# A gated-MLP kernel after linear attention: one written order of steps replaced by another

## The chip, the core and the metric

One core of a Trainium2 chip runs the whole program. Its engines are TensorE (PE, matmuls), VectorE (DVE), ScalarE (ACT), GpSimd (POOL) and SyncE (SP), which issues every DMA here. The metric is device time of one execution in microseconds, lower is better.

## What is computed

Eight batches of 576 rows. The first half is attention without a score matrix: q is made a softmax over its 64 channels, k one over the 576 rows, k^T v is a 64x64 matrix for each of 8 heads, and x = q (k^T v). The second half is a gated MLP with a mixing of rows:

```python
kv = einsum('bhsd,bhse->bhde', softmax(k, axis=rows), v)
x = einsum('bhsd,bhde->bhse', softmax(q, axis=channels), kv)   # heads side by side: 576 x 512
h = gelu_tanh(x @ w_in)                                        # 576 x 1024
u, v = h[..., :512], h[..., 512:]
v_n = (v - mean(v)) / sqrt(var(v) + 1e-6) * g_ln
gated = u * (einsum('ts,bsd->btd', w_sg, v_n) + b_sg[None, :, None])
out = x + gated @ w_out
```

## The kernel before

Each large product is made in float32r from a high and a low part of each operand: three matmuls (high x high, low x high, high x low) that add up in PSUM. So every operand has a step that rounds it to the high part (ScalarE mostly) and one that subtracts to get the low part (VectorE or GpSimd).

The work is cut into 1167 small steps, and a text, PLAN (lines 46 to 133 from the point that matters here), lists them with their arguments: batch first, then tile, head or part, and a letter where the engine is chosen (V VectorE, A ScalarE, G GpSimd). A loop at the end calls them in that order, each by its name. Nothing else sets the order: `InOrder` (line 141) ties every instruction of VectorE, ScalarE, GpSimd and SyncE to the one before it on the same engine, and `mm` keeps TensorE's matmuls in the order of the text. Between engines there are only the waits that data and buffers need. A step that waits holds up everything behind it on its own engine.

The steps that this document speaks of, with the line of each:

- load_q, load_k, load_v, load_kt (387 to 399): DMA loads of one part of a batch. kt_max, kt_put, kt_get (402 to 415): the maxima of k over the rows, written to DRAM and read back in every partition. The loads of kt and kt_get take turns in two buffers (5 b + p, modulo 2).
- k_sub, k_exp (419, 425): k less its maxima, and the exponential. q_max, q_swapm, q_top, q_sub, q_exp, q_sum, q_swapd, q_inv, q_mul, q_turn (504 to 636): softmax of q and its transposition. q_max, q_top, q_sum, q_inv and q_turn are VectorE's.
- x_kv (685): first x_mm of a batch, 32 matmuls in three PSUM tiles, then kv_all of the next batch, whose matmuls read k and v; x_high, x_low, x_endh, x_endl (730 to 742) read the three tiles; kv_inv and kv_scale (671, 676) read kv_all's.
- hv_mm (747), hv_gelu, hv_sq, hv_stat, hv_pow, hv_norm, hv_high, hv_low (757 to 790): a 128-row tile of v, its GELU, its norm, high and low part. tail_high, tail_low, tail_again (799 to 808): the last 64 rows of a batch.
- hu_mm, hu_gelu (813, 818): one quarter of u. sg_mm (821), 28 matmuls: the mixing of rows for one quarter, which reads the high and low part of v of all tiles, in order. gate, gate_high, gate_low (830 to 837): u times that, its high and low part.
- out_mm (850), out_add, out_rest, out_store (856 to 866): the last product, the addition of x's high and low part, and the store. last_mm and what follows (873): the last quarter of the last batch in three column groups.
- wo_a, wo_b, wo_d, wo_h, wo_l (297 to 317) and ws_h, ws_l, b_h, b_l: the weights' high and low parts, w_out put together from 64-bit words by a scale, a shift and an OR. The raw words of w_out lie in the buffers that x_h and x_l of batch 1 take later.

PSUM has three double tiles that x_mm, hu_mm, sg_mm, out_mm and last_mm take in turn and two single ones for hv_mm and kv_all (`bank`, line 225). A step of the first kind cannot begin until the tile of three turns ago has been read: by gate on VectorE after a sg_mm, by out_add on VectorE after an out_mm, by hu_gelu on ScalarE after a hu_mm.

Of the kernel before, what the change touches and what calls it, by code (L numbers as in the profile page):

```python
# [59 lines left out]
hv_stat 1 0 A, hv_stat 1 1 A, q_sub 2 1, q_exp 2 1, gate 0 2, load_k 2 0, k_sub 2 0, hv_stat 1 2 A, hv_pow 1 2, q_sum 2 1, k_exp 2 0, sg_mm 0 0  # L60
gate 0 0, q_swapd 2 1, q_inv 2 1, q_mul 2 1 1, q_mul 2 1 0, sg_mm 0 1, hv_high 1 2, gate_high 0 2, load_kt 3 1, hu_mm 1 0, k_exp 2 1, kv_all 2
load_k 3 0, load_kt 3 2, hv_pow 1 0, gate 0 1, gate_high 0 1, gate_high 0 0, hv_stat 1 3, hv_pow 1 3, gate_high 0 3, hv_norm 1 3, gate_low 0 0
gate_low 0 1, gate_low 0 2, gate_low 0 3 G, q_max 2 0, hu_gelu 1 0, out_mm 0 1, hv_norm 1 0, wo_l 2 V, kt_max 3 1, kt_max 3 2, load_k 3 1, q_swapm 2 0
# [68 lines left out]
out_add 7 1, out_store 7 1, both 7 0, out_mm 7 0, out_add 7 0, out_store 7 0, last_mm 7 1, out_mm 7 2, out_add 7 2, last_add 7 1, out_store 7 2
last_store 7 1, last_mm 7 0, last_mm 7 2, last_add 7 0, last_store 7 0, last_add 7 2, last_store 7 2
"""


# [821 lines left out]
```

## Time and profile before

| | |
|---|---|
| median of 3 runs | 495.99 us (495.83 to 497.17) |
| profiled execution | 497.11 us, span 495.3 us, granted TensorE clock 1.0 throughout |
| TensorE matmul | 485.9 us busy, 98% of the span, 3885 matmuls |
| TensorE weight load | 447.3 us, 90% |
| VectorE | 338.9 us, 68%, 530 instructions |
| ScalarE | 244.4 us, 49% |
| GpSimd | 159.5 us, 32%, 173 instructions |
| DMA | 57.28 MB, mean 116 GB/s |

The engines' busy times overlap; idle time of an engine costs only where it holds up the one that ends last. Matmuls are pipelined, so each is shown longer (295 ns for 288 columns) than the distance to the next start (some 133 ns); a stop of TensorE is read from the starts, or from the idle time in brackets, which is shorter.

### The profile page before, as it was taken

What the parts mean: (1) busy time and instruction counts of PE and PEld (TensorE: products, weight loads), DVE (VectorE), ACT (ScalarE), POOL (GpSimd) and SP (SyncE); (2) the same over time, 40 slices, a digit from 0 to 9 for tenths busy, and PEclk for the clock granted to TensorE, in tenths of its full rate; (3) what the DMA queues carried; (4) which work ended last, traced back from release to release, by engine and by line L of the source; (5) the groups of instructions that cost most, each with busy time, mean ns of one, the idle gap of its engine ahead of it and who ended that gap; (6) DMA issues with size and microseconds to landing.
All of it is one profiled execution on the core that took longest, in us unless ns stands there. A gap on an engine that the chain in (4) does not pass through costs nothing.

```text
span 495.3 us, 9376 instructions
## 1 busy us (share of the span) xinstructions
PE 485.9 (98%) x3885; PEld 447.3 (90%) x3885; DVE 338.9 (68%) x530; ACT 244.4 (49%) x402; POOL 159.5 (32%) x173
## 2 busy tenths in 40 slices
...
GB/s 301 386 406 194 285 52 120 148 61 145 175 228 55 192 218 85 71 103 26 179 48 201 97 194 11 78 125 1 119 26 0 25 73 0 1 1 24 32 42 96
DMA packets 20637, 57.28 MB, mean 116 GB/s; under 512 B 3057, under 2 KB 3569, under 8 KB 20594
## 3 DMA queue, kind: packets, MB, share of 16 engines
...
q8 instruction: 30, 0.49, 0.4%
...
## 4 chain that ended last, share of the span: by engine, by line
PE 66%; DVE 14%; DMA 8%; POOL 5%; issue 3%; ACT 3%; SPq 1%; POOLq 0%; ACTq 0%; DVEq 0%
PE ps L238 66%; DVE o L151 2%; DMA kmt<-kt 2%; DVE qq L151 2%; DMA vv<-v 2%; DMA qq<-q 2%; DVE qd L151 2%; POOL qq L151 2%; POOL kk L151 1%; DVE qm L151 1%; DMA out<-o 1%; DMA eye<-identity 1%; ACT qq L151 1%; DVE vnl L151 1%; POOL o L151 1%
## 5 line engine op out<-in xcount | busy, mean ns | idle before, releaser
L238 PE MATMUL ps<-ulow,wo_h 128*128 128x288 f32 (+1 forms) x260 | 56.8, 296 | 0.5 <-DVE ulow L151 0.5
L238 PE MATMUL ps<-gh,wo_h 128*128 128x288 f32 (+1 forms) x260 | 56.6, 295 | 0.3 <-DVE o L151 0.3
L238 PE MATMUL ps<-gh,wo_l 128*128 128x288 f32 (+1 forms) x260 | 56.2, 293 | 0.0
L238 PE MATMUL ps<-ws_h,vnh 128*128 128x288 f32 x256 | 55.0, 296 | 0.0
L238 PE MATMUL ps<-ws_h,vnl 128*128 128x288 f32 x256 | 54.8, 295 | 0.0
L238 PE MATMUL ps<-ws_l,vnh 128*128 128x288 f32 x256 | 54.8, 295 | 0.0
L151 POOL TENSOR_TENSOR ulow<-u,gh 128x576 fp32r<-128x576 f32 x16 | 25.0, 1560 | 83.0 <-DVE ulow L151 53.8
L151 POOL TENSOR_TENSOR rs<-ve,half 128x1 f32<-128x1 f32 x36 | 25.9, 723 | 77.2 <-DVE ve L151 71.0
L151 ACT CAST gh<-u 128x576 fp32r<-128x576 f32 x32 | 20.9, 673 | 58.7 <-DVE u L151 58.6
L151 ACT ACT_TABLE_LOAD x34 | 43.6, 1283 | 9.7 <-PE ps L238 4.3
L151 DVE TENSOR_TENSOR u<-ps,u 128x576 f32<-128x576 f32 x32 | 23.8, 748 | 32.3 <-PE ps L238 32.3
L238 PE MATMUL ps<-x_h,wi_h 128*128 128x288 f32 (+2 forms) x256 | 42.1, 299 | 1.6 <-DVE o L151 1.3
L238 PEld LDWEIGHTS ps<-gh,wo_h 128*128 128x128 f32 x260 | 42.1, 188 | 1.1 <-DVE o L151 0.5
L238 PEld LDWEIGHTS ps<-ulow,wo_h 128*128 128x128 f32 x260 | 42.0, 188 | 0.9 <-DVE ulow L151 0.9
L238 PEld LDWEIGHTS ps<-ws_h,vnh 128*128 128x128 f32 x256 | 41.7, 188 | 0.7
L238 PEld LDWEIGHTS ps<-gh,wo_l 128*128 128x128 f32 x260 | 42.1, 188 | 0.0
L151 ACT ACTIVATE u<-ps 128x576 f32<-128x576 f32 (+2 forms) x36 | 21.0, 597 | 42.7 <-PE ps L238 39.0
L238 PEld LDWEIGHTS ps<-ws_h,vnl 128*128 128x128 f32 x256 | 41.3, 188 | 0.0
L238 PE MATMUL ps<-x_h,wi_l 128*128 128x288 f32 (+2 forms) x256 | 41.3, 296 | 0.0
L238 PEld LDWEIGHTS ps<-ws_l,vnh 128*128 128x128 f32 x256 | 41.3, 188 | 0.0
L238 PE MATMUL ps<-x_l,wi_h 128*128 128x288 f32 (+2 forms) x256 | 41.2, 295 | 0.0
L238 PE MATMUL ps<-wi_h,x_h 128*128 128x512 f32 x144 | 39.9, 399 | 0.6 <-ACT x_h L151 0.5
...
## 6 DMA issues: line engine op xcount, KB each, us to landing
...
```

The source lines that it names most:

```text
L151: ins = op(*args, **kw)
L238: tc.keep_in_program_order(nc.tensor.matmul(*args, **kw))
```

## The change

The text of PLAN is written anew from the 180th step on. The 179 steps ahead of it stay as they are, up to the first matmuls that transpose k of batch 1. The steps are the same 1167, each with the same arguments and the same engine; only their order differs, and with it the order of each engine's instructions. The words that came with it: order of the steps from batch 1's k^T v on made anew, with VectorE's two-SBUF-input instructions and GpSimd taking turns in order of time; nothing else. No wait or dependency is written into the kernel for that.

The diff has 90 lines of steps on either side. Those that this document speaks of:

```diff
@@ -46,91 +46,91 @@
-k0_copy 1 2, q_turn 1 2, hu0_mm 0 1 1, hu0_mm 0 1 0, k0_copy 1 3, hu0_gelu 0 1, ws_h 0, kv_mm 1 0, load_v 2 0, kv_inv 1 0, hu0_gelu 0 0, kv_mm 1 1
-load_k 2 1, kv_scale 1 0, kv_inv 1 1, kv_scale 1 1, load_q 2 1, x_mm 1, wo_b 0, wo_d 0, x_high 1 1, x_endh 1, wo_b 2, hv_pow 0 3, load_w_sg 2, wo_d 2
-x_endl 1, x_low 1 1, hv_high 0 3, ws_l 0, load_b, x_high 1 0, hv_mm 0 1, x_low 1 0, hv_gelu 0 1, hv_sq 0 2, hv_stat 0 2 A, hv_pow 0 2, hv_norm 0 2
...
-hv_low 0 1, hv_stat 0 4 A, wo_h 0, hv_pow 0 4, load_kt 2 2, kt_max 2 2, hv_norm 0 4, tail_high 0, kt_max 2 3, kt_put 2, ws_l 2 V, kt_get 2
...
-hv_sq 1 2, hv_norm 1 2, wo_h 2, k_sub 2 1, kt_max 3 0, b_l, sg_mm 0 3, sg_mm 0 2, q_swapm 2 1 G, q_top 2 1, gate 0 3, hv_gelu 1 0 A, hv_sq 1 0
...
-out_rest 0 3 V, q_mul 2 0 1, load_v 3 0, hu_mm 1 2, hu_gelu 1 2, kv_scale 2 0, k_sub 3 0, q_turn 2 2, sg_mm 1 0, load_q 3 1, gate 1 0, k_sub 3 1 G
...
-q_turn 2 1, hu_mm 1 1, hu_gelu 1 1, load_kt 4 3, kt_max 4 3, load_q 3 0, sg_mm 1 2, gate 1 2, k_exp 3 0, out_store 0 3, kt_put 4, q_max 3 0
-q_swapm 3 0, out_store 0 0, q_swapm 3 1 G, q_top 3 0, q_sub 3 0, sg_mm 1 1, gate 1 1, k_exp 3 1, gate_high 1 1, gate_low 1 1 G, gate_high 1 2
...
-q_swapm 4 1 G, q_top 4 1, load_v 4 1, hu_mm 2 1, hu_gelu 2 1, hv_stat 2 3 A, hv_pow 2 3, x_kv 3, x_high 3 0, x_low 3 0, kv_inv 4 0, kv_scale 4 0
...
-hv_gelu 3 2 A, q_max 4 0, tail_low 2, q_swapm 4 0 G, q_top 4 0, load_v 5 0, q_sub 4 0 V, hu_gelu 2 0, q_mul 4 1 1, q_exp 4 0, q_sum 4 0, out_store 1 1
...
-out_mm 2 3, out_add 2 3, out_rest 2 3 V, out_add 2 1, q_swapm 5 1 G, q_top 5 1, hv_pow 3 3, hv_gelu 3 0, hv_stat 3 0, load_v 5 1, hv_norm 3 3
-hv_high 3 3, hv_low 3 3, out_mm 2 0, out_rest 2 1, q_top 5 0, q_sub 5 0 V, q_exp 5 0, out_mm 2 2, out_add 2 2, hv_pow 3 0, out_add 2 0, out_rest 2 0 V
-hv_stat 3 2 A, hu_mm 3 1, hv_norm 3 0, hu_gelu 3 1, hu_mm 3 3, hu_gelu 3 3, x_kv 4, load_k 6 1, hv_norm 3 1, load_v 6 0, hv_high 3 0, out_rest 2 2 V
...
-out_store 4 2, hu_gelu 5 1, hu_mm 5 3, hu_gelu 5 3, hv_low 5 1, sg_mm 5 1, q_mul 6 1 1 V, q_turn 6 3, q_sum 7 0, gate 5 1, sg_mm 5 0, gate_high 5 1
...
-x_endl 6, out_store 4 3, sg_mm 5 3, gate 5 3, q_swapd 7 0 G, q_inv 7 0, load_q 7 1, gate_high 5 3, kv_inv 7 1, kv_scale 7 1, gate_low 5 0 G
...
-out_mm 5 1, q_top 7 1, q_sub 7 1, q_turn 7 0, out_store 4 0, q_exp 7 1, hv_mm 6 3, hv_stat 6 1, q_sum 7 1, q_swapd 7 1, q_inv 7 1, hv_norm 6 1
...
-last_store 7 1, last_mm 7 0, last_mm 7 2, last_add 7 0, last_store 7 0, last_add 7 2, last_store 7 2
...
+k0_mm 1 3, k0_copy 1 3, hu0_mm 0 0 1, wo_b 0, hu0_mm 0 0 0, hu0_mm 0 1 1, hu0_mm 0 1 0, kt_max 2 0, q_turn 1 3, kv_mm 1 0, load_v 2 0, wo_d 0
+kv_inv 1 0, kv_scale 1 0, hv_gelu 0 0 A, hv_sq 0 0, q_turn 1 2, k0_copy 1 2, kv_mm 1 1, kv_inv 1 1, kv_scale 1 1, hv_sq 0 2, load_kt 2 1
+hv_stat 0 2 A, load_v 2 1, ws_h 0, hu0_gelu 0 1, load_q 2 0, hv_norm 0 2, hv_stat 0 0 A, hv_pow 0 0, wo_b 2, hu0_gelu 0 0, wo_d 2, hv_norm 0 3, x_mm 1
+x_high 1 0, x_endh 1, x_endl 1, x_high 1 1, x_low 1 1, x_low 1 0, hv_high 0 3, kt_max 2 1, hv_low 0 3, hv_mm 0 1, hv_gelu 0 1, hv_pow 0 2, ws_h 2
+hv_high 0 2, hv_stat 0 1, hv_low 0 2, hv_norm 0 0, hv_mm 0 4, hv_gelu 0 4 A, hv_sq 0 4, hv_stat 0 4 A, hv_norm 0 4, hv_high 0 0, hv_low 0 0
+hv_norm 0 1, ws_l 0, ws_l 2 V, load_q 2 1, hv_mm 1 3, hv_gelu 1 3, load_k 2 1, load_kt 2 3, kt_max 2 3, hv_pow 0 4, tail_high 0, load_kt 2 2
+hv_mm 1 1, kt_max 2 2, hv_gelu 1 1 A, hv_pow 0 1, load_w_sg 4, ws_h 4 V, ws_l 4 V, load_b, b_h, tail_high 1, tail_low 1, hv_high 0 1, hv_low 0 1
+tail_again 0, tail_low 0, wo_h 2, wo_l 2 V, hv_mm 1 0, hv_gelu 1 0 A, hv_mm 1 2, q_max 2 0, b_l, sg_mm 0 0, q_max 2 1, q_swapm 2 1 G, load_kt 3 0
...
+load_q 3 0, q_max 3 0, k_sub 3 0, q_turn 2 3, load_q 3 1, kv_scale 2 1, q_swapm 3 0, hu_gelu 1 2, sg_mm 1 0, gate 1 0, gate_high 1 0, gate_low 1 0
+sg_mm 1 2, gate 1 2, gate_high 1 2, k_sub 3 1 G, kt_max 4 2, q_max 3 1, q_swapm 3 1 G, sg_mm 1 1, gate 1 1, out_store 0 2, q_top 3 1, sg_mm 1 3
...
+x_endl 2, out_add 1 2, q_sum 3 1, q_swapd 3 1 G, q_turn 3 1, load_v 4 1, q_mul 3 0 0, hv_gelu 2 3 A, q_inv 3 1, q_mul 3 1 1, out_rest 1 2 V
...
+out_store 1 0, k_exp 5 1, out_add 2 0, out_rest 2 0 V, out_store 1 3, out_mm 2 3, out_add 2 3, q_swapm 5 1 G, hv_sq 3 2, q_top 5 1, q_sub 5 1
+out_mm 2 1, load_q 5 0, q_max 5 0, out_store 1 1, out_add 2 1, out_rest 2 1, q_exp 5 1, hv_stat 3 2 A, hv_norm 3 2, kt_max 6 0, q_swapm 5 0
+hv_pow 3 0, q_top 5 0, out_store 1 2, out_mm 2 2, load_kt 6 1, out_add 2 2, out_rest 2 2 V, load_kt 6 2, kt_max 6 1, load_kt 6 3, hu_mm 3 1
+hu_gelu 3 1, hu_mm 3 3, hu_gelu 3 3, load_v 5 0, x_kv 4, x_high 4 0, load_v 6 1, hv_high 3 3, load_k 6 0, hv_stat 3 1, hv_norm 3 1, out_rest 2 3 V
...
+out_store 2 1, kv_inv 5 0, kv_scale 5 0, x_endh 4, x_endl 4, q_sum 5 1, kv_scale 5 1, q_sub 5 0 V, hv_high 3 2, hv_low 3 2, hu_mm 3 2, q_exp 5 0
...
+gate 5 3, gate_high 5 0, x_endh 6, gate 5 2, gate_low 5 0 G, gate_high 5 1, gate_low 5 1, gate_high 5 2, gate_low 5 2 G, x_endl 6, hv_mm 6 3
+hv_gelu 6 1, hv_stat 6 1, hv_pow 6 1, gate_high 5 3, hu_mm 6 0, gate_low 5 3, out_mm 5 2, hu_gelu 6 0, q_sum 7 1, q_swapd 7 1, q_inv 7 1, q_mul 7 1 0
...
+out_rest 6 2, hu_gelu 7 1, hv_low 7 0, out_store 6 2, hv_high 7 3, tail_again 7, hv_low 7 3, sg_mm 7 1, gate 7 1, sg_mm 7 0, gate 7 0, gate_high 7 0
...
+out_add 7 0, out_store 7 0, out_store 7 1, out_mm 7 2, both 7 2, last_store 7 0, out_add 7 2, out_store 7 2, last_mm 7 1, last_mm 7 2, last_add 7 1
+last_store 7 1, last_add 7 2, last_store 7 2
```

## Rows read from the trace of the kernel before

**Rows 1.** Busy time by stretch, 50 to 75 us; columns in the first line

```profile
core 0: us, PE busy (x) PEld busy (x) DVE busy (x) ACT busy (x) POOL busy (x), PEclk, DMA share, GB/s
50.00:75.00 25.00, 24.47 (x195) 19.13 (x192) 22.72 (x36) 18.20 (x37) 11.10 (x11) 1.00 0.52 169
```

**Rows 2.** Timeline, TensorE: start us, us, engine line op out<-in xcount [idle before]

```profile
57.62 1.21 PE L238 MATMUL ps<-wi_h,x_h 128*128 128x512 f32 x4 [0.53 <-ACT x_h L151]
...
71.95 0.43 PE L238 MATMUL ps<-ws_h,vnh 128*128 128x288 f32 x2
...
132.75 1.32 PE L238 MATMUL ps<-qt,kvt 64*64 64x512 f32 x24 [1.47 <-DVE u L151]
...
169.46 2.36 PE L238 MATMUL ps<-vv,kk 64*64 64x65 f32 x72 [0.22 <-DMA vv<-v]
...
217.13 0.54 PE L238 MATMUL ps<-gh,wo_h 128*128 128x288 f32 x2 [0.29 <-DVE o L151]
...
221.48 1.23 PE L238 MATMUL ps<-x_h,wi_l 128*128 128x288 f32 x8
222.55 1.23 PE L238 MATMUL ps<-x_l,wi_h 128*128 128x288 f32 x8
225.07 1.20 PE L238 MATMUL ps<-x_h,wi_h 128*128 128x288 f32 x7 [1.29 <-DVE o L151]
...
375.39 0.53 PE L238 MATMUL ps<-ulow,wo_h 128*128 128x288 f32 x2 [0.45 <-DVE ulow L151]
```

**Rows 3.** Timeline, VectorE around x_kv 2

```profile
129.45 1.35 DVE L151 TENSOR_REDUCE qm<-qq 128x36 f32<-128x1152 f32 x1 [2.35 <-DMA qq<-q]
...
131.95 1.42 DVE L151 TENSOR_TENSOR u<-ps,u 128x576 f32<-128x576 f32 x2
```

**Rows 4.** Timeline, GpSimd and VectorE ahead of hu_mm 3 3

```profile
219.50 2.13 POOL L151 TENSOR_TENSOR qq<-qq,qm 128x1152 f32<-128x1152 f32 x1
...
219.98 2.21 DVE L151 SCALAR_TENSOR_TENSOR vnl<-v,rs,vnh 128x512 fp32r<-128x512 f32 x1 [0.85 <-ACT vnh L151]
...
223.60 1.42 DVE L151 TENSOR_TENSOR o<-ps,x_h 128x576 f32<-128x576 f32 x2
```

**Rows 5.** Groups by form, VectorE: busy us, mean ns of one, idle before

```profile
L151 DVE SCALAR_TENSOR_TENSOR vnl<-v,rs,vnh 128x512 fp32r<-128x512 f32 x32 | 25.9, 820 | 7.4 <-ACT vnh L151 7.3
```

**Rows 6.** Timeline, VectorE, 52 to 75 us

```profile
52.63 2.03 DVE L151 TENSOR_SCALAR o<-o 128x1024 uint32<-128x1024 uint32 x1
54.69 1.23 DVE L151 SCALAR_TENSOR_TENSOR o<-raw_x_h,o 128x1024 uint32<-128x1024 uint32 x1
55.84 0.69 DVE L151 TENSOR_SCALAR o<-o 128x1024 uint32<-128x1024 uint32 x1
...
57.92 3.02 DVE L151 TENSOR_TENSOR x_l<-ps,x_h 128x256 fp32r<-128x256 f32 x4
...
61.57 0.75 DVE L151 SCALAR_TENSOR_TENSOR vnl<-v,rs,vnh 128x512 fp32r<-128x512 f32 x1
...
67.78 0.74 DVE L151 SCALAR_TENSOR_TENSOR vnl<-v,rs,vnh 128x512 fp32r<-128x512 f32 x1
...
70.49 2.20 DVE L151 TENSOR_TENSOR ws_l<-ghws,ws_h 128x1280 fp32r<-128x1280 f32 x1
...
73.50 0.49 DVE L151 CAST ws<-ghws 128x640 fp32r<-128x640 f32 x1
74.03 0.82 DVE L151 TENSOR_TENSOR ws<-ghws,ws 64x640 fp32r<-64x640 f32 x1
```

**Rows 7.** Timeline, GpSimd, 51 to 72 us

```profile
51.20 2.91 POOL L151 TENSOR_TENSOR ws_l<-ghws,ws_h 128x1280 fp32r<-128x1280 f32 x1 [0.62 <-ACT ws_h L151]
...
64.70 0.56 POOL L151 TENSOR_TENSOR rs<-ve,half 128x1 f32<-128x1 f32 x1 [2.63 <-DVE ve L151]
...
69.30 2.04 POOL L151 TENSOR_TENSOR ws<-ghws,ws 1x640 fp32r<-1x640 f32 x1
```

**Rows 8.** Loads of v: time of an issue on SyncE in ns, and to landing

```profile
L151 SPq DMA_DIRECT2D vv<-v x16: 327/426/736, 6.6 to 310.2; - x16
...
DMA to landing us min/median/max: 3.9/6.7/9.8
```

More of the change, by code (lines that the diff above doesn't have):

```diff
@@ L60 @@
[L60 to L63, printed above, removed]
@@ L100 @@
-hv_high 4 2, hv_high 4 0, out_store 3 0, hv_low 4 0, q_turn 5 2, q_turn 5 3, load_q 6 1, k_exp 6 1, out_add 3 3, out_rest 3 3 V, out_mm 3 1
-out_add 3 1, hv_low 4 2, hu_mm 4 3, hu_gelu 4 3, x_kv 5, x_high 5 0, load_k 7 1, hv_pow 4 3, q_max 6 1, out_rest 3 1, x_low 5 0, kv_inv 6 0
-out_store 3 1, q_swapm 6 1, hu_mm 4 2, x_high 5 1, hv_high 4 3, kt_max 7 0, q_top 6 1, kv_inv 6 1, kv_scale 6 1, q_top 6 0, kv_scale 6 0, x_endh 5
-q_sub 6 0, hu_gelu 4 2, q_exp 6 0, load_kt 7 2, x_endl 5, x_low 5 1, hv_mm 4 4, q_sub 6 1 V, hv_low 4 1, hv_low 4 3, q_exp 6 1, q_sum 6 1, hv_mm 5 2
@@ L120 @@
-out_mm 5 3, hu_gelu 6 1, hv_norm 6 0, hv_high 6 1, hv_stat 6 3 A, out_add 5 3, out_rest 5 3 V, out_rest 5 0, x_kv 7, x_high 7 1, out_rest 5 1
-x_endh 7, x_endl 7, x_high 7 0, x_low 7 0, hv_low 6 1, hv_pow 6 3, hv_mm 6 2, hv_gelu 6 2, out_store 5 0, hv_high 6 3, hv_stat 6 2, hv_mm 6 4
-hv_norm 6 2, x_low 7 1, hu_mm 6 2, hv_pow 6 2, hv_high 6 2, hv_low 6 2, hv_mm 7 1, hv_gelu 6 4, hv_mm 7 0, hv_stat 6 4, hv_norm 6 4, hv_pow 6 4
-tail_high 6, tail_low 6, tail_again 6, out_store 5 1, hv_low 6 3, hv_high 6 0, hv_low 6 0, hu_gelu 6 2, hv_gelu 7 1, sg_mm 6 2, gate 6 2
@@ L132 @@
[L132 to L133 removed]
+load_w_sg 0, hv_gelu 0 3, wo_a 2, k0_mm 1 0, k0_mm 1 1, hv_stat 0 3, load_w_out 0, q_mul 1 0 0 V, q_swapd 1 1 G, load_g, load_w_sg 2, k0_mm 1 2
+k0_copy 1 1, k0_copy 1 0, load_w_sg 1, q_inv 1 1, hv_pow 0 3, q_turn 1 1, hv_mm 0 0, q_mul 1 1 1, wo_a 0, q_turn 1 0, q_mul 1 1 0, hv_gelu 0 2 A
```

117 lines of the change are left out of this document (62 added, 55 removed).

## The prediction

> **What bounds the kernel now.** I read the busy table by stretches first. From 50 to 75 us, right behind the point where the orders part, TensorE is busy 24.5 of 25 us, VectorE 22.7 and GpSimd 11.1 [rows 1]. TensorE is the bound, with VectorE close behind, and the change neither adds nor removes one of its matmuls, so only the places where it stands still can be won. I looked for those in TensorE's timeline: after the point where the two orders part (the 180th of 1167 steps) it stops visibly six times [rows 2], for 0.53, 1.47, 0.22, 0.29, 1.29 and 0.45 us by the idle time in the brackets. That undercounts a little: eight matmuls of hu_mm take 1.07 us from start to start (221.48 to 222.55), so that the next start was due at 223.62 and came at 225.07, which is 1.45 where the bracket says 1.29. With 0.16 more for each of six, all of them come to 4.25 + 0.96 = 5.2 us. That is the most that any order can gain here, 1.0% of the time. The profile was taken in an execution of 497.11 us (span 495.3); the median of the runs is 1.12 lower, and I sum in the former and take the 1.12 off at the end.
>
> **Why TensorE stops: an engine's queue is in order.** The stop of 1.47 us is inside x_kv 2, which takes the three PSUM tiles that sg_mm 1 2, 1 1 and 1 3 wrote. VectorE's queue has q_max 3 0 ahead of gate 1 1. q_max 3 0 waited 2.35 us for its load, and the two gates that free the tiles began at 131.95 though their matmuls were done long before [rows 3]. The stop of 1.29 us (hu_mm 3 3) waits for out_add 2 0, second of the pair at 223.60, and ahead of that stands hv_low 3 3 with 2.21 us [rows 4].
>
> **What the change's rule is about.** That hv_low is the clearest row of the contention. GpSimd's q_sub 5 1 ran from 219.50 for 2.13 us, to 221.63; hv_low 3 3 began at 219.98 and ended at 222.19, 0.56 after GpSimd let go [rows 4]. A free hv_low takes 0.75 [rows 6], and the mean of all 32 is 820 ns [rows 5]. So the two do not share, one waits for the other's whole instruction; out_add, with one of its inputs in PSUM, keeps its 0.71 (two in 1.42). The premise is sound. A slower VectorE costs something only where TensorE waits for it, though, and that is the 5.2 us.
>
> **Stops that the new order takes away.** (1) x_kv 2: load_q 3 0 used to stand behind hu_mm 1 1 and load_kt 4 3; now both loads of q go out before sg_mm 1 0, q_max 3 0 runs before any gate of batch 1, and between gate 1 2 and gate 1 1 stand kt_max 4 2 and q_max 3 1, about 2.1 us of work against 3.73 of the sg_mm beside it. Gone: 1.47 + 0.16. (2) x_kv 3: its stop waited for a DMA of v [rows 2]; load_v 4 1 now goes out around out_mm 1 3, some 20 us ahead. Gone: 0.38. (3) out_mm 2 2 and hu_mm 3 3: each out_add of batch 2 now stands close behind its own out_mm (at most hv_stat, hv_norm, kt_max and q_top between), and q_sub 5 0 V comes only after x_kv 4. Gone: 0.45 + 1.45. (4) out_mm 5: before, one hv_mm stands between the last sg_mm 5 and the first out_mm 5, which waited for ulow; now hv_mm 6 3 and hu_mm 6 0 stand there. Gone: 0.61. What hides each chain is now a step of 2.8 to 3.7 us; without it the old price is back. Together 4.5 us.
>
> **The front, first place: no gain taken.** The stop at 57.62 comes from x_endh 1, which sits behind x_high 1 1, which waits for wo_d 0, the reader of its buffer; wo_b 0 ahead of that took 2.03 us against 0.69 for wo_b 2 [rows 6], because GpSimd's ws_l 0 held from 51.20 for 2.91 [rows 7]. In the new order wo_b 0 and wo_d 0 come before kv_mm 1 0, so that this wait goes. But other work now stands ahead of x_endl 1. VectorE was through with kv_scale 1 1 when wo_b 0 began, at 52.63; from there come wo_b 2 (0.69), wo_d 2 (1.23, as wo_d 0), hv_norm 0 2 and 0 3 (0.75 each, like the other two-input instructions of 512 columns) and two short ones of 0.15 (an estimate), so that x_endl 1 begins at 56.4. It is 1.3 later if wo_b 0 meets a q_mul of GpSimd as it met ws_l 0 (2.03 - 0.69), and 2.9 later if ws_l 0 gets in front. x_endl 1 takes some 0.8, and hv_mm 0 4 wants it at about 57.8. So the place costs between nothing and 2.3 (56.4 + 2.9 + 0.8 - 57.8); I leave it at the 0.69 that it costs now.
>
> wo_b is a tensor_scalar with one SBUF input, and that row shows it blocked too. The Trainium skill, "SBUF — State Buffer", section "Who interferes with whom", says so: copy, cast and tensor_scalar can enter a two-port mode and then contend with GpSimd like instructions with two SBUF inputs. The trace agrees (2.03 against 0.69), and that rule speaks against this change, whose rule has two-input instructions alone. By the page wo_b 0 and ws_h 4 V still collide, and x_endl 1 begins 1.3 later than by the change's own rule, by which they don't; either way the place stays inside its bounds.
>
> **The front, second place: a new wait.** The first sg_mm needs hv_low 0 1 after its first eight matmuls. Before, hv_low 0 1 ended at 68.52, far ahead of the need at about 73.0 (the first sg_mm began at 71.95 [rows 2], and 1.07 on). The new order puts ahead of it ws_l 2 V (2.20), ws_h 4 V (0.49), ws_l 4 V (0.82), and tail_low 1, hv_norm 0 0, hv_norm 0 4 and two more kt_max (five at about 0.75); it takes q_max 2 1 (1.35, as q_max 3 0 in [rows 3]) and hv_norm 0 2 (0.75) away [rows 6]. That is 7.26 - 2.10 = 5.2 us more. From the start of x_endl 1 (57.92) to the end of hv_low 0 1 it was 10.6 us, so now 15.8 at most. Begun at 56.4 to 57.7, it ends at 72.2 to 73.5, and up to 6.6 later if ws_l 0 (2.91), b_l (2.04) and three hv_pow (0.56 each) [rows 7] all get in the way. The stall is between nothing and 7.1 us. Most of what is ahead is reductions, statistics and PSUM readers, which do not collide, so I take a value near the low end: 0.8.
>
> **A load that comes late.** load_v 5 0 used to go out well before the x_kv 4 that needs it, between q_top 4 0 and q_sub 4 0. Now it stands last in SyncE's queue before x_kv 4, behind load_kt 6 3, which waits until kt_max 6 1 has read its buffer; kt_max 6 1 follows out_add 2 2 and out_rest 2 2 V. From the end of out_mm 2 2: three VectorE instructions of 0.75 and an issue of load_kt 6 3 (an issue takes 0.43 [rows 8]) make 2.7 us. The matmuls on v come two hu_mm (3.2 each) and an x_mm (24 of its 32 matmuls take 1.32 [rows 2], so 1.8) later, 8.2. So it has 5.5 us to land, where loads of v take 3.9 to 9.8, median 6.7 [rows 8]. The cost is between nothing and 4.3. At the median it is 1.2; DMA traffic is lighter there than in the front, so I take 1.0. Queued behind load_v 5 0 is nothing that is needed soon.
>
> **The rest** of the moved steps, hu_mm against hv_mm, the order of sg_mm and out_mm within a batch, the stores, and the last out_mm and last_mm, I cost at nothing: TensorE's sum is the same, and added up on their engines the producers end before they are needed. The closest is hv_low 7 3: hu_gelu 7 1, hv_high 7 3 and itself, three of some 0.75, after hu_mm 7 1, against the twenty matmuls (2.67) of sg_mm 7 1 ahead of its use, which leaves 0.4. The tail still ends in out_mm 7 2, last_mm 7 1 and last_mm 7 2. Where a cover fails, it costs one instruction, 0.75 on VectorE.
>
> **Sum.** -4.5 + 0.8 + 1.0 = -2.7 us. 497.1 - 2.7 = 494.4 profiled, less 1.12: 493.3.
>
> **Rivals.** (a) Clean: the front gains as well and the load lands in time: -5.2, 490.8. For it: VectorE's busy share falls. Against it: the two new orders of service above, which I could price at nothing only at their best ends. 0.14. (b) Nothing won: order on paper isn't order on the chip. The list fixes each engine's own sequence and puts no wait between VectorE and GpSimd, so GpSimd starts whatever has its inputs. ws_l 0 stands late in the list, and yet only hv_pow 0 0 and 0 2 keep it back. If such meetings stay as many as before, the two new waits are about 2 us each: -4.5 + 4.0 = -0.5, 495.5, between 494.5 and 497.5. 0.20. (c) Slower: GpSimd in the front. ws_l 0, b_l and the hv_pow each stand in front of a two-input instruction before hv_low 0 1, which ends at 80.1 instead of 73.0. The first sg_mm then loses 7.1 us that a busy TensorE never gets back, and the net is -4.5 + 7.1 + 1.0 = +3.6, 499.6. The gain is used up once hv_low 0 1 ends after 76.5, and from 78.0 on the kernel is slower by over 0.3%. For it: VectorE is busy 22.7 of 25 us there [rows 1] and has 5.2 us more to do. Against it: of the 15.8 us of work less than half has two inputs in SBUF. 0.18.
>
> **Numbers.** The forecast, 491.8 to 494.4, has 0.48. About 0.3% (1.5 us) is what a measurement of this kernel can tell from no change; faster than 494.5 are the forecast and (a), 0.62; (b) is the same, 0.20; (c) slower, 0.18. The range from 490.3 to 498.3 takes in the forecast, (b), most of (a) and the near part of (c).
>
> **What would show it.** In the changed profile TensorE has no stop in x_kv 2, x_kv 3, hu_mm 3 3 and the first out_mm 5; the mean of hv_low falls from 820 toward 750 ns. A stop inside the first sg_mm, with VectorE as releaser, shows the second place of the front, and one at the first vv matmul of x_kv 4, released by a DMA of v, shows the load. I am wrong if TensorE stops for more than 3 us in sum at places that I cost at nothing, or if the stops of x_kv 2 and hu_mm 3 3 stay.

## The result, and the profile of the changed kernel

The changed kernel takes 490.76 us (median of 4 runs, 490.68 to 491.71) against 496.58 of the kernel before on the same chip (495.83 to 497.37): ratio 0.9887, interval [0.9864, 0.9910]. Two later series of the same kernel gave 0.9902 [0.9887, 0.9916] and 0.9891 [0.9861, 0.9922]. Between the two profiled executions (497.11 and 491.71) the time falls by 5.4 us, between the medians of the three series by 5.8, 5.1 and 4.8, where 2.7 were forecast. That is inside the range from 490.3 to 498.3, but below the forecast's own 491.8 to 494.4, and it is what the rival "clean" had said (490.8, with a chance of 0.14).

The busy table of the changed kernel's page (engine, busy us, share of the span, instructions):

```profile
span 489.9 us, 9391 instructions
PE 483.5 (99%) x3885; PEld 446.9 (91%) x3885; DVE 334.8 (68%) x530; ACT 240.3 (49%) x398; POOL 162.2 (33%) x173
```

TensorE is busy for 99% where it was 98%. Since the brackets undercount, I compare steps: from the first start of a step to the first start of the next one on TensorE, in both traces. Added up, from the first matmul to the last, they give the 5.4 us by which the span fell.

| step of TensorE | before | after | forecast for it | measured |
|---|---|---|---|---|
| x_kv 2 | 6.33 | 4.36 | -1.63 | -1.97 |
| x_kv 3 | 4.81 | 4.36 | -0.38 | -0.45 |
| out_mm 2 0, 2 2, hu_mm 3 1, 3 3 | 14.97 | 12.85 | -1.90 | -2.12 |
| out_mm 5 1 | 3.90 | 3.17 | -0.61 | -0.73 |
| hv_mm 0 1, 0 4 (front, first place) | 6.68 | 5.72 | 0 | -0.96 |
| first sg_mm (front, second place) | 3.73 | 3.73 | +0.8 | 0 |
| x_kv 4 (load_v 5 0) | 4.36 | 4.36 | +1.0 | 0 |
| sg_mm 1 0 | 3.73 | 4.68 | 0 | +0.95 |
| all others (the largest of the changed part -0.30, in out_mm 7 1) | | | 0 | -0.1 |
| sum | | | -2.7 | -5.4 |

TensorE's timeline of the changed kernel at the places of [rows 2]: x_kv 2 and x_kv 3 run through, hu_mm 3 1 is followed by hu_mm 3 3 without a stop, the first out_mm 5 gets its ulow in time, hv_mm 0 4 (57.20) begins on time, and so do the first sg_mm's matmuls on hv_low 0 1 (72.27) and x_kv 4's on v (225.99); the one bracket behind the point where the orders part is that of sg_mm 1 0.

```profile
57.20 1.10 PE L238 MATMUL ps<-wi_h,x_h 128*128 128x512 f32 x4
...
72.27 0.42 PE L238 MATMUL ps<-ws_h,vnl 128*128 128x288 f32 x2
...
116.11 0.53 PE L238 MATMUL ps<-ws_h,vnl 128*128 128x288 f32 x2 [0.67 <-DVE vnl L151]
...
130.17 2.18 PE L238 MATMUL ps<-qt,kvt 64*64 64x512 f32 x32
132.17 2.43 PE L238 MATMUL ps<-vv,kk 64*64 64x65 f32 x80
...
167.01 2.43 PE L238 MATMUL ps<-vv,kk 64*64 64x65 f32 x80
...
219.63 1.23 PE L238 MATMUL ps<-x_l,wi_h 128*128 128x288 f32 x8
220.70 1.23 PE L238 MATMUL ps<-x_h,wi_h 128*128 128x288 f32 x8
...
225.99 2.43 PE L238 MATMUL ps<-vv,kk 64*64 64x65 f32 x80
...
388.63 0.42 PE L238 MATMUL ps<-ulow,wo_h 128*128 128x288 f32 x2
```

The groups of hv_low and of VectorE's k_sub in the changed kernel (busy us, mean ns of one), and behind them k_sub's in the kernel before:

```profile
L151 DVE SCALAR_TENSOR_TENSOR vnl<-v,rs,vnh 128x512 fp32r<-128x512 f32 x32 | 30.9, 972 | 14.9 <-ACT vnh L151 14.7
L151 DVE TENSOR_TENSOR kk<-kk,kmt 128x1280 f32<-128x1280 f32 x8 | 11.8, 1475 | 0.0
```

```profile
L151 DVE TENSOR_TENSOR kk<-kk,kmt 128x1280 f32<-128x1280 f32 x8 | 17.8, 2239 | 2.4 <-DMA kmt<-scr 2.4
```

k_sub no longer meets GpSimd at all (1475 ns; a single free one took 1.48 us), but hv_low, expected to fall from 820 [rows 5] toward 750, rose to 972. Four of its 32 carry nearly all of that (3.55, 1.97, 2.62 and 1.91 us), and only the first of them stops TensorE, in sg_mm 1 0. The meetings of the two engines have moved more than they have gone.

### The profile page after: what moved, and what is told of

It is laid out like the page before. It is cut to its first block, busy times and chain, and to the rows that moved or that the text cites. A ratio compares the mean times of both kernels' runs of the same rounds, so it can differ in the third digit from the quotient of the medians.

```text
span 489.9 us, 9391 instructions
## 1 busy us (share of the span) xinstructions
PE 483.5 (99%) x3885; PEld 446.9 (91%) x3885; DVE 334.8 (68%) x530; ACT 240.3 (49%) x398; POOL 162.2 (33%) x173
## 4 chain that ended last, share of the span: by engine, by line
PE 92%; DVE 4%; ACT 2%; issue 1%; DMA 1%; POOL 0%; ACTq 0%
PE ps L238 92%; DVE o L151 1%; DVE vnl L151 1%; DMA qq<-q 1%; ACT qq L151 1%; DVE wi_l L151 0%; ACT qs L151 0%; DVE qm L151 0%; ACT x_l L151 0%; DVE qq L151 0%; POOL qq L151 0%; ACT o L151 0%; DVE wi_h L151 0%; DVE qd L151 0%; DVE qt L151 0%
## 5 line engine op out<-in xcount | busy, mean ns | idle before, releaser
L238 PE MATMUL ps<-gh,wo_l 128*128 128x288 f32 (+1 forms) x260 | 56.4, 294 | 0.0
L151 POOL TENSOR_TENSOR rs<-ve,half 128x1 f32<-128x1 f32 x36 | 27.9, 780 | 50.6 <-DVE ve L151 50.2
L151 DVE SCALAR_TENSOR_TENSOR vnl<-v,rs,vnh 128x512 fp32r<-128x512 f32 x32 | 30.9, 972 | 14.9 <-ACT vnh L151 14.7
```

Source lines behind the costliest of these rows:

```text
L151: ins = op(*args, **kw)
L238: tc.keep_in_program_order(nc.tensor.matmul(*args, **kw))
```

## The experiments

**First set: is it the order of the queues, or the meetings with GpSimd?** My first theory followed the prediction: six late producers stand behind something else in their queue, and freeing them is the whole gain.

Five places by hand, in the order of before (only the moved steps are shown):

```diff
 hu0_mm 0 1 1, hu0_mm 0 1 0, k0_copy 1 3, hu0_gelu 0 1, ws_h 0
+wo_b 0, wo_d 0
 kv_mm 1 0
...
 k_exp 3 0, out_store 0 3, kt_put 4
-q_max 3 0, q_swapm 3 0, q_swapm 3 1 G, q_top 3 0, q_sub 3 0
 sg_mm 1 1, gate 1 1, k_exp 3 1, gate_high 1 1, gate_low 1 1 G, gate_high 1 2, sg_mm 1 3, gate 1 3
+q_max 3 0, q_swapm 3 0, q_swapm 3 1 G, q_top 3 0, q_sub 3 0
...
 out_mm 1 0, load_k 4 1
+load_v 4 1
...
+out_add 2 1
 out_add 2 3, out_rest 2 3 V
...
+out_mm 2 0, out_add 2 0
 hv_low 3 3
...
+hv_mm 6 3
 out_mm 5 1
```

> The order of before, with only those steps moved that stand ahead of one of the six stops: q_max 3 0, its swap, q_top and q_sub behind gate 1 3; out_add 2 1 ahead of out_add 2 3 and out_rest 2 3, and out_mm 2 0 with out_add 2 0 ahead of hv_low 3 3; wo_b 0 and wo_d 0 ahead of kv_mm 1 0; load_v 4 1 behind load_k 4 1; hv_mm 6 3 ahead of out_mm 5 1. No two-input instruction is placed by GpSimd's time. Theory (the gain is the head of a queue freed at six places): by the differences of TensorE's steps between the two traces, 1.97 (x_kv 2), 1.46 and 0.46 (hu_mm 3 1, out_mm 2 0), 0.68 and 0.28 (hv_mm 0 1, hv_mm 0 4), 0.45 (x_kv 3) and 0.73 (out_mm 5 1), 6.0 us in all, so 490.6 against 496.6 of before, 489.9 to 492.0. Rival (the gain comes from fewer meetings of VectorE and GpSimd over the whole kernel): those stay as they are but for wo_b 0, at most 1 us is won, 495.5 or more.

Measured 493.36 (493.24 to 494.66), ratio 0.9950 [0.9934, 0.9966]: 2.85 won, half of what the theory expected and more than the rival allowed. The steps that were aimed at lost 1.46 (hu_mm 3 1), 0.45 (out_mm 2 0), 0.72 (out_mm 5 1), 0.45 (x_kv 3) and 1.00 (front), but x_kv 2 only 0.79, and 0.76 and 0.78 came back in kv_mm 1 1 and x_kv 4. TensorE's stops there, and VectorE's timeline ahead of the first:

```profile
52.77 2.18 PE L239 MATMUL ps<-qt,kvt 64*64 64x512 f32 x32 [0.69 <-DVE kr L152]
...
226.37 1.32 PE L239 MATMUL ps<-qt,kvt 64*64 64x512 f32 x24 [0.55 <-ACT u L152]
```

```profile
50.12 0.65 DVE L152 TENSOR_SCALAR o<-o 128x1024 uint32<-128x1024 uint32 x1
50.81 1.22 DVE L152 SCALAR_TENSOR_TENSOR o<-raw_x_h,o 128x1024 uint32<-128x1024 uint32 x1
51.95 0.15 DVE L152 TENSOR_SCALAR kr<-ps 128x2 f32<-128x2 f32 x1
```

The moved wo_b 0 and wo_d 0 now make kv_inv 1 0 late (51.95), for which x_mm 1 waits. hv_low 3 3 still takes 2.20 us, though hu_mm 3 1 no longer waits for it; behind it q_sub 5 0 on VectorE is late, so q_exp 5 0 on ScalarE, and so hu_gelu 3 1, for which x_kv 4 waits. What is moved out of one wait lengthens the next.

GpSimd's in-place work cut to a strip, in both orders:

```diff
-        E.tensor_tensor(out=k4, in0=k4, in1=top.broadcast_to(k4.shape), op=ALU.subtract)
+        if E is G:
+            k4, top = k4[:, 0:1, :, 0:8], top[:, :, :, 0:8]
+        E.tensor_tensor(out=k4, in0=k4, in1=top.broadcast_to(k4.shape), op=ALU.subtract)
...
-        o = o_s(b, e)
+        n = 32 if E is G else S
+        o = o_s(b, e)[:, 0:n]
```

> The order of before; GpSimd's k_sub, q_sub, q_mul and out_rest of the later batches work on a strip of their columns alone, so that part of the computation is left out and VectorE hardly meets GpSimd there. Theory: of the six stops only those whose late producer was stretched by GpSimd go, the 1.46 of hu_mm 3 1 (hv_low 3 3 under q_sub 5 1) and little else: those of x_kv 2 and x_kv 3 wait for loads, those of the front meet ws_l, and out_mm 5 1 waits for gate_low on GpSimd itself. 495.1, 494.0 to 496.0. Rival (meetings are what the order of before costs): nearly the whole 5.6 us is won without touching the order, 491 to 492.

> The new order with the same strip of columns for GpSimd's k_sub, q_sub, q_mul and out_rest (part of the computation is left out). Theory: the 0.94 us of the stop in sg_mm 1 0, where hv_low 1 1 waited 3.55 us beside k_sub 3 1, goes and nothing else, 489.8, 489.2 to 490.6; the distance to the same kernel in the old order stays at some 5 us. Rival: with the meetings gone the order hardly matters, and the two differ by 1.5 us or less.

Measured 491.72 (491.59 to 492.16), ratio 0.9916 [0.9901, 0.9930], for the old order, and 490.72 (490.66 to 490.75), ratio 0.9894 [0.9879, 0.9908], for the new. My theory had said 495.1 for the first; the rival had said 491 to 492. With GpSimd's work short, x_kv 2 falls to 4.36, hu_mm 3 1 to 3.20, out_mm 5 1 to 3.17 and x_kv 3 to 4.36 without a step being moved; only the front keeps its 0.97. And the two orders are 1.0 us apart, as the rival of the second text had it; that text's 489.8 did not come, though the stop in sg_mm 1 0 went (3.73 us), for a reason that the third set bears out: the 490.8 that it started from lies at the lower of two levels, which that stop seems to part. The busy tables of the two, the old order first:

```profile
PE 483.7 (99%) x3885; PEld 446.6 (91%) x3885; DVE 323.4 (66%) x530; ACT 244.5 (50%) x402; POOL 99.9 (20%) x173
```

```profile
PE 483.7 (99%) x3885; PEld 447.0 (91%) x3885; DVE 320.8 (66%) x530; ACT 240.2 (49%) x398; POOL 110.0 (22%) x173
```

VectorE's instructions are the same 530. GpSimd's strips take 338.9 - 323.4 = 15.5 us of waiting out of them in the old order and 334.8 - 320.8 = 14.0 in the new one. So the new order does not have much less meeting in it; it has it elsewhere.

One meeting put back into the new order's front:

```diff
-hv_norm 0 1, ws_l 0, ws_l 2 V, load_q 2 1, hv_mm 1 3, hv_gelu 1 3, load_k 2 1, load_kt 2 3, kt_max 2 3, hv_pow 0 4, tail_high 0
+hv_norm 0 1, ws_l 2 V, load_q 2 1, hv_mm 1 3, hv_gelu 1 3, load_k 2 1, load_kt 2 3, kt_max 2 3, hv_pow 0 4, ws_l 0, tail_high 0
```

> The new order with one step moved: GpSimd's ws_l 0 behind hv_pow 0 4, so that it begins at about 64.8 instead of 56.0 and lies beside ws_l 2 V. Tests the price of the slower case named ahead of the result. If a meeting in the front is paid in full: ws_l 2 V ends 2.5 us later (held until 67.8, then 1.2), hv_low 0 1 ends at 74.3 instead of 71.7, needed at 72.3, so the first sg_mm stops for 2.0 us (1.0 to 2.6) and the time is 492.8 (491.8 to 493.5). If VectorE has room there that takes it up: no stop and 490.8.

Measured 493.19 (493.11 to 494.72), ratio 0.9950 [0.9935, 0.9966]: 2.4 us more than the 490.76 of the changed kernel, by one GpSimd instruction at another time. GpSimd's, VectorE's and TensorE's timelines, and the granted clock behind the stop (columns as in [rows 1]):

```profile
63.87 3.25 POOL L153 TENSOR_TENSOR ws_l<-ghws,ws_h 128x1280 fp32r<-128x1280 f32 x1
```

```profile
64.23 3.45 DVE L153 SCALAR_TENSOR_TENSOR v<-v,mv,g_bc 128x512 f32<-128x512 f32 x1
...
73.78 0.75 DVE L153 SCALAR_TENSOR_TENSOR vnl<-v,rs,vnh 128x512 fp32r<-128x512 f32 x1
```

```profile
74.59 0.54 PE L240 MATMUL ps<-ws_h,vnl 128*128 128x288 f32 x2 [2.03 <-DVE vnl L153]
```

```profile
74.00:76.00 2.00, 1.41 (x7) 1.41 (x8) 1.94 (x3) 1.28 (x5) 0.00 (x0) 0.76 0.84 99
76.00:78.00 2.00, 2.00 (x10) 2.00 (x9) 2.00 (x3) 1.94 (x9) 0.00 (x0) 0.50 0.89 352
78.00:80.00 2.00, 2.00 (x15) 2.00 (x15) 2.00 (x5) 1.90 (x5) 0.72 (x4) 0.89 0.00 0
```

It was hv_norm 0 1, not ws_l 2 V, that met ws_l 0: 3.45 us instead of 0.74, ended at 67.68, 0.56 after GpSimd. The stop of 2.0 us is the one expected. In this execution (494.72) the granted clock fell behind it to 0.50, the lower level (1.2 GHz), and the step of TensorE took 7.80 instead of 3.73. Two of six times lie at 494.6 to 494.7 and four at 493.1 to 493.2; that the clock is what parts them is likely, since the mean granted clock over the execution was 0.995 in those two and 0.998 to 0.999 in the four, but only one was profiled.

**Second set: which meetings?** The new theory: a stop's first cause is a VectorE instruction held up by GpSimd, and the wait for a load or a gate that the profile names is the end of the chain. For x_kv 2 the suspect is k_sub 3 0, in the kernel before (VectorE, then GpSimd's k_sub 3 1 and out_rest 0 1):

```profile
112.88 4.03 DVE L151 TENSOR_TENSOR kk<-kk,kmt 128x1280 f32<-128x1280 f32 x1
```

```profile
112.11 3.45 POOL L151 TENSOR_TENSOR kk<-kk,kmt 128x1280 f32<-128x1280 f32 x1
115.52 2.68 POOL L151 TENSOR_TENSOR o<-o,x_l 128x576 f32<-128x576 f32 x1
```

```diff
+        if (b, h) == (3, 1):
+            k4, top = k4[:, 0:1, :, 0:8], top[:, :, :, 0:8]
         E.tensor_tensor(out=k4, in0=k4, in1=top.broadcast_to(k4.shape), op=ALU.subtract)
...
+        if (b, h) == (5, 1):
+            q3, top = q3[:, 0:1], top[:, 0:1]
```

> The order of before; of GpSimd's 173 instructions two, k_sub 3 1 and q_sub 5 1, work on a strip of their columns alone (that part of the computation is left out). Neither result is waited for by a stop of TensorE; what changes is that VectorE's k_sub 3 0 (4.03 us in before) and hv_low 3 3 (2.21) no longer meet them. New theory (the first cause of x_kv 2's stop is that meeting: k_sub 3 0 late, so load_kt 4 1, kt_max 4 1, q_turn 2 1, load_q 3 0, q_max 3 0 and gate 1 1 late): x_kv 2 loses its 1.97 and hu_mm 3 1 its 1.46, out_mm 2 0 keeps its 0.46; 492.8 (492.2 to 494.0). Rival (the stop of x_kv 2 comes from the order of the loads and of q_max 3 0 in their queues): only 1.46 is won, 494.8.

> The order of before with the two strips of the earlier run and a third, out_rest 0 1 on GpSimd (that part of the computation is left out): with k_sub 3 1 a strip, k_sub 3 0 still met out_rest 0 1, took 2.69 us instead of 1.48, and x_kv 2 kept 0.67 of its stop. Theory: k_sub 3 0 takes 1.5, x_kv 2 loses the last 0.67, 493.2 against 493.9 of the two strips (492.8 to 493.7). Rival: what is left of the stop comes from the queues, 493.9.

Measured 493.86 (493.58 to 494.23), ratio 0.9951 [0.9936, 0.9966], with two strips (inside its range, 1.1 above the 492.8 expected; 0.67 of that is what x_kv 2 kept, since out_rest 0 1 still met k_sub 3 0) and 493.19 (492.94 to 493.89), ratio 0.9945 [0.9930, 0.9960], with the third (`n = 32 if (b, e) == (0, 1) else S` in out_rest). k_sub 3 0 and x_kv 2 on TensorE, with two strips and then with three:

```profile
112.36 2.69 DVE L152 TENSOR_TENSOR kk<-kk,kmt 128x1280 f32<-128x1280 f32 x1
...
130.00 2.42 PE L239 MATMUL ps<-qt,kvt 64*64 64x512 f32 x32
```

```profile
112.17 1.48 DVE L152 TENSOR_TENSOR kk<-kk,kmt 128x1280 f32<-128x1280 f32 x1
...
129.88 2.18 PE L239 MATMUL ps<-qt,kvt 64*64 64x512 f32 x32
```

k_sub 3 0 got 1.34 us shorter and x_kv 2 lost 1.30 (5.03); then 1.21 shorter again, and it lost the remaining 0.67 (4.36). hu_mm 3 1 lost 1.44 in both. The chain between them can be followed on VectorE: kt_max 4 1 and q_turn 2 1 in the kernel before, and then with two strips, where both come 1.3 us earlier (k_sub 3 0 ended 1.86 earlier there: 1.34 by its length, 0.52 because it began earlier in that execution).

```profile
122.17 0.75 DVE L151 TENSOR_REDUCE ktall<-kmt 128x1 f32<-128x576 f32 x1 [0.69 <-DMA kmt<-kt]
...
124.11 0.77 DVE L151 STREAM_TRANSPOSE qt<-qq 128x576 f32<-128x576 f32 x1
```

```profile
120.83 0.75 DVE L152 TENSOR_REDUCE ktall<-kmt 128x1 f32<-128x576 f32 x1 [1.04 <-DMA kmt<-kt]
...
122.76 0.77 DVE L152 STREAM_TRANSPOSE qt<-qq 128x576 f32<-128x576 f32 x1
```

This is shown, then: without three GpSimd instructions, on none of whose results one of these stops waits, the steps of TensorE lose 1.97 + 1.44 = 3.4 us in the old order. By the medians the three strips are worth 3.0 us: the steps are taken from the one profiled execution of the kernel before, which at 497.11 lies 0.9 above the median of this series (496.21).

A few moves again, better chosen (those of the front, of load_v 4 1 and of hv_mm 6 3 are in the text below alone):

```diff
-q_max 3 0, q_swapm 3 0, q_swapm 3 1 G, q_top 3 0, q_sub 3 0
...
 x_kv 2, load_v 4 0, x_high 2 0, x_endh 2, x_low 2 0, x_high 2 1
+q_max 3 0, q_swapm 3 0, q_swapm 3 1 G, q_top 3 0, q_sub 3 0
...
+out_add 2 1
 out_add 2 3, out_rest 2 3 V
...
-q_sub 5 1
...
 q_exp 5 1, hu_mm 3 0, kv_inv 5 0, hv_pow 3 2
+q_sub 5 1
```

> The order of before with a few steps moved, chosen so that no moved step stands ahead of anything that the moves of the first experiment held up: q_max 3 0, its swaps, q_top and q_sub behind x_high 2 1; GpSimd's q_sub 5 1 behind hv_pow 3 2, so that hv_low 3 3 runs free; out_add 2 1 ahead of out_add 2 3; load_v 4 1 behind load_k 4 1; hv_mm 6 3 ahead of out_mm 5 1; wo_b 0 and wo_d 0 ahead of kv_mm 1 0 with hv_norm 0 0 behind kv_scale 1 1. Theory (six places are all that the order costs): 1.97 + 1.46 + 0.46 + 0.45 + 0.73 + 0.97 = 6.0 us are won, 490.2 against 496.2 (489.8 to 491.5). Rival (the two-input instructions must take turns with GpSimd over the whole kernel, or the lateness comes back at the next place): 492.5 or more, with stops of over 1.5 us at places that before does not have.

(q_exp 5 1 comes before q_sub 5 1 here, so the exponential of that half of batch 5 is taken of values without their maxima off.) Measured 496.31 (495.97 to 498.43), ratio 1.0012 [0.9998, 1.0026]: nothing won, as its rival had it and worse. The front, x_kv 3, out_mm 2 0 and out_mm 5 1 gained what they should; x_kv 2 kept 6.28, hu_mm 3 1 kept 4.78, and out_mm 1 1 took 1.8 more. TensorE, and then VectorE and GpSimd ahead of hu_mm 3 1:

```profile
133.30 2.36 PE L239 MATMUL ps<-vv,kk 64*64 64x65 f32 x72 [1.69 <-DMA vv<-v]
...
139.25 0.54 PE L239 MATMUL ps<-ulow,wo_h 128*128 128x288 f32 x2 [1.52 <-POOL ulow L152]
```

```profile
217.50 1.42 DVE L152 TENSOR_TENSOR qm<-qm,qs 128x36 f32<-128x36 f32 x1
...
221.44 0.75 DVE L152 SCALAR_TENSOR_TENSOR vnl<-v,rs,vnh 128x512 fp32r<-128x512 f32 x1 [0.85 <-ACT vnh L152]
```

```profile
217.14 1.73 POOL L152 TENSOR_TENSOR o<-o,x_l 128x576 f32<-128x576 f32 x1
```

Behind the gates of x_kv 2 stands a second late one, load_v 3 1, which lands when the gates used to come: freeing the gates alone gives nothing here, and gave 0.79 in the first run by hand. And hv_low 3 3 runs free now (0.75), but q_top 5 1, an instruction of 36 columns, met out_rest 2 1 instead (1.42; it takes 0.19 when free), everything behind it came later, and hu_mm 3 1 stopped as before. out_mm 1 1 waits for a gate_low that now stands behind the moved q_sub 3 0 on GpSimd.

**Third set: the load, and the new stop.** load_v 5 0 went out at 221.19 in the changed kernel and landed at 225.43, 0.56 ahead of the matmul at 225.99. Made later:

```diff
 out_add 2 2, out_rest 2 2 V, load_kt 6 2
+hv_stat 3 1, hv_norm 3 1
 kt_max 6 1, load_kt 6 3
```

> The new order with hv_stat 3 1 and hv_norm 3 1 ahead of kt_max 6 1: load_kt 6 3 and behind it load_v 5 0 go out about 1.7 us later (222.9 instead of 221.2). In the new kernel that load landed 4.24 us after its issue, 0.56 before the matmul on it began. If the term ahead of the result was right in kind (a late load is paid past that margin): landed at 227.1, a stop of 1.1 us in x_kv 4, 491.9 (490.7 to 493.5, for landings of 3.9 to 6.7). If the place has another cover: 490.7.

Measured 492.32 (491.81 to 493.53), ratio 0.9933 [0.9916, 0.9951]. The load went out at 221.86 and landed 4.17 later; x_kv 4 took 5.48, 1.12 more, as expected:

```profile
226.07 2.48 PE L240 MATMUL ps<-vv,kk 64*64 64x65 f32 x80 [0.89 <-DMA vv<-v]
```

The stop in sg_mm 1 0 comes from hv_low 1 1, held up by k_sub 3 1. VectorE and GpSimd in the changed kernel, where two hv_low take 4.29 together, and then in the kernel with the late load, whose order is the same up to 214 us:

```profile
111.77 4.29 DVE L151 SCALAR_TENSOR_TENSOR vnl<-v,rs,vnh 128x512 fp32r<-128x512 f32 x2
```

```profile
112.54 2.96 POOL L151 TENSOR_TENSOR kk<-kk,kmt 128x1280 f32<-128x1280 f32 x1 [2.97 <-issue]
```

```profile
111.93 1.40 DVE L153 SCALAR_TENSOR_TENSOR vnl<-v,rs,vnh 128x512 fp32r<-128x512 f32 x2
```

```profile
114.69 2.96 POOL L153 TENSOR_TENSOR kk<-kk,kmt 128x1280 f32<-128x1280 f32 x1 [5.17 <-PE ps L240]
```

In the text of the changed kernel k_sub 3 1 G stands behind gate_high 1 2. On the chip it starts when kt_get 3 lands: 112.42 in the first trace (issued 108.54), 114.57 in the second (issued 109.86), where it came too late for hv_low 1 1 (it met the end of k_sub 3 0 alone, 1.78 us instead of 1.48) and there is no stop. So a load that lands earlier goes with a stop here, and no wait forbids it. To test that the meeting is the cause, hv_low 1 1 was moved ahead:

```diff
-hu_gelu 1 3, hv_pow 1 1, kt_get 3, out_add 0 3, q_mul 2 0 0 V, q_turn 2 0, out_rest 0 1, out_rest 0 3 V, kv_scale 2 0, hv_high 1 1, hv_low 1 2, hv_low 1 1
+hv_pow 1 1, hv_high 1 1, hu_gelu 1 3, kt_get 3, out_add 0 3, q_mul 2 0 0 V, q_turn 2 0, hv_low 1 1, out_rest 0 1, out_rest 0 3 V, kv_scale 2 0, hv_low 1 2
```

> The new order with three steps moved: hv_pow 1 1 and hv_high 1 1 ahead of hu_gelu 1 3, for which hv_high 1 1 waited on ScalarE, and hv_low 1 1 directly behind q_turn 2 0, so that it runs before GpSimd's k_sub 3 1 begins. Theory (a meeting costs only where the stretched instruction is the last one that TensorE waits for): the stop of 0.94 us in sg_mm 1 0 goes, and since it is the only stop left behind the point where the orders part, the gain is 0.94, 489.8 against 490.8 (489.4 to 490.3). Rival: k_sub 3 1 then meets another two-input instruction and the 0.94 comes back elsewhere, 490.8.

> The new kernel once more, unchanged. Of its four first times one was 491.71 (the profiled one, with a stop of 0.94 us in sg_mm 1 0) and three 490.68 to 490.78. Theory: that stop is no fixture, since no wait ties k_sub 3 1 to hv_low 1 1; most executions run without it, the median is 490.7, and if the profile catches one of them sg_mm 1 0 takes 3.73 us. Rival: the stop is in every execution, the times lie at 491.7 again or the profile shows sg_mm 1 0 with 4.7 us at a time of 490.7.

> The new kernel, unchanged, beside the one with hv_high 1 1 early, on one chip. Theory (the stop in sg_mm 1 0 is there when kt_get 3 lands ahead of hv_low 1 1, since k_sub 3 1 then starts at once, and is absent when it lands later): single times at two levels, about 490.8 and 491.6, median between 490.7 and 491.6; in the profile a stop of 0.8 to 1.0 us if k_sub 3 1 begins by 112.6, none if after 113.4. Rival (no connection): stop and start of k_sub 3 1 don't go together.

> The new order with hv_pow 1 1, hv_high 1 1 and hv_low 1 1 early, beside the new kernel on one chip. Theory: hv_low 1 1 is through before k_sub 3 1 can begin, whenever kt_get 3 lands, so the times lie at one level, 490.6 (490.4 to 491.0), without that stop: 0 to 1.0 us ahead of the new kernel's median, 0.5 at even shares. Rival: as many of its times as the new kernel's lie above 491.2.

With hv_low 1 1 ahead, measured 490.62 (490.51 to 491.01), ratio 0.9888 [0.9871, 0.9904], and on the chip of the last pair 490.77 (490.67 to 491.14), ratio 0.9880 [0.9854, 0.9905], against 491.63 (490.98 to 491.88) of the changed kernel beside it; the changed kernel took 491.13 (490.81 to 491.55) in the series between. The first of these texts missed: the stop went, but the time was its rival's 490.8 and not 489.8, because three of the changed kernel's first four times had been low ones. The second, by which most executions run without the stop, missed as well: half of its four times were high. The last two held, but for at most 0.14 us. The twelve single times of the changed kernel lie at two levels, six from 490.68 to 490.98 and six from 491.42 to 491.88; all eight of the improved one lie between 490.51 and 491.14. In its first trace k_sub 3 1 began at 112.37, as early as ever, and sg_mm 1 0 took 3.73: hv_low 1 1 was through, and hv_low 1 2 had begun. (In its second trace k_sub 3 1 began at 114.88 and tests nothing.) VectorE's timeline of the first, and GpSimd's k_sub 3 1 in it:

```profile
110.67 0.71 DVE L153 SCALAR_TENSOR_TENSOR vnl<-v,rs,vnh 128x512 fp32r<-128x512 f32 x1
...
112.16 0.74 DVE L153 SCALAR_TENSOR_TENSOR vnl<-v,rs,vnh 128x512 fp32r<-128x512 f32 x1
```

```profile
112.37 3.35 POOL L153 TENSOR_TENSOR kk<-kk,kmt 128x1280 f32<-128x1280 f32 x1 [3.06 <-issue]
```

In all three traces of the changed kernel k_sub 3 1 began by 112.8 (112.73 in the last, just behind the 112.6 of its text) and the stop was there (0.95, 0.83, 0.90); in two other kernels with the same order around that place, the one with the late load and the one with ws_l 0 late, k_sub 3 1 began after both hv_low had ended, and it was not. That the lower of the two levels, some 0.8 apart, is that of the executions without the stop is what this suggests; it is not shown, since all three profiled executions of the unchanged kernel lie at the upper one.

## Why the prediction was right, and where it was not

**Right.** TensorE was the bound and only its stops could be won. All four items that were written off at 4.5 us went, for 5.27. The 0.75 more is the estimate of a stop: bracket plus 0.16 misses what follows the stop inside the step (in x_kv 2 the matmuls on v also came late, 2.70 us for 80 instead of 2.43). The first out_mm 5 and x_kv 3 came out within 0.12. For the same reason 5.2 us was no ceiling: the six places gave 6.2. The gain came out at twice the forecast because four terms were off to the same side (0.75 here, and 0.96, 0.8 and 1.0 below) and only one to the other (0.95). That the rival "clean" hit the number is partly luck: it had neither the 6.2 nor the 0.95.

**Mis-sized: the front, first place.** It was left at its 0.69, with bounds from nothing to 2.3; it went, for 0.96. The start of x_endl 1 was estimated at 56.4 and measured at 56.20, so the step was right and the choice inside its bounds was not; hv_mm 0 4 began at 57.20, not at the 57.8 that the bound of 2.3 went by. ws_l 0 did run there, but beside instructions with an input in PSUM:

```profile
56.20 3.01 DVE L151 TENSOR_TENSOR x_l<-ps,x_h 128x256 fp32r<-128x256 f32 x4
```

```profile
56.00 3.11 POOL L151 TENSOR_TENSOR ws_l<-ghws,ws_h 128x1280 fp32r<-128x1280 f32 x1
```

Four of them, 3.01 us, none stretched. (That an input in PSUM keeps an instruction out of the way the prediction read from out_add in [rows 4], which had no GpSimd instruction beside it; these four show it.) wo_b 0 did meet a q_mul, as feared, but it had begun first: it took 0.73, and the q_mul 1.61 where the one before it took 1.16. The other instruction that had been named there did collide: ws_h 4 V, a cast with one input, took 1.57 at 67.71 against 0.49 [rows 6], under b_l. The section "Who interferes with whom" of "SBUF — State Buffer" in the Trainium skill, which counts copies and casts among the instructions that contend, has this trace on its side for that one.

**Mis-sized: the first sg_mm.** Priced at 0.8, measured 0: hv_low 0 1 ended at 71.69, a little ahead of the estimated 72.2 to 73.5, and was wanted at 72.27. The 2.20 of ws_l 2 V in that sum was itself the time of a meeting, with b_l [rows 6, 7]; free, it took 1.49. The danger was real all the same: one GpSimd instruction placed elsewhere gave a stop of 2.0 and 2.4 us of time, close to the whole forecast gain. So the slower rival was right in kind, and the place of ws_l 0 alone is enough to bring its stop about; a stop near its 7.1 was not seen.

**Mis-sized: load_v 5 0.** Priced at 1.0 from a median landing of 6.7 [rows 8] against 5.5 us of room; the room was 4.8, but it landed in 4.24, near the shortest of them, with 0.56 to spare. Made 0.67 later against a TensorE that is 1.0 earlier, it cost 1.12: right in kind, wrong in the landing time.

**Wrong: a place costed at nothing.** sg_mm 1 0 stops for 0.95 in the profile and, as the times suggest, in half of the executions. That is the mechanism of rival (b): the list puts no wait between VectorE and GpSimd.

**Half the cause: why the stops were there.** The prediction took x_kv 2's stop for a matter of queues (load_q 3 0 behind other loads, q_max 3 0 ahead of gate 1 1) and wrote that a slower VectorE costs something only where TensorE waits for it. That sentence is true, but I looked for such places one step back from TensorE only. k_sub 3 0 stands some ten steps back: it makes load_kt 4 1 late, that kt_max 4 1, q_max 3 1 and q_turn 2 1, that load_q 3 0, that q_max 3 0, and that the gate. In the old order the 1.97 us all hang on the meetings of k_sub 3 0 (with k_sub 3 1, and with out_rest 0 1 once that one is short); of hu_mm 3 1's stop 1.44 on one meeting of hv_low 3 3, which the prediction did see. The order of the queues is a condition beside the meeting: at hu_mm 3 1 the moves of the first run took 1.46 away with hv_low 3 3 still at 2.20. At x_kv 2 the queues that the prediction names were not enough: behind them load_v 3 1 was late too (1.69 in the run with few moves), which its item (1) does not have. That the new order also issues load_v 3 1 far earlier, at 88.74 instead of 127.35, is luck as far as the prediction goes. The repairs by hand were made for the queues, and won 2.85 and nothing. So meetings, which the change's rule is about, do bear on most of what the old order lost. Whether the new order took x_kv 2's stop away by its free k_sub 3 0 (1.48) or by its queues, no run parts. The expected sign, a lower mean of hv_low, was the wrong sign: which instructions meet counts, and the mean rose while the time fell.

**Open.** In out_mm 5 1 (0.73) and x_kv 3 (0.45) the strips shortened GpSimd's own work as well as the meetings, and no run parts the two. x_kv 3's stop also went when only instructions some 50 us earlier were cut, so it may hang on when a transfer happens to land; it is seen in one profiled execution of the kernel before, and that kernel's single times reach from 495.16 to 498.87.
